# Later reads of the experts' names, a first matrix loaded in two halves, and more dummy products in a routed expert layer

## The chip, the core and the metric

The kernel runs on one core of one Trainium2 chip. Five engines work on their own instruction queues: PE (TensorE, matrix products), DVE (VectorE), ACT (ScalarE), POOL (GpSimd) and SP (SyncE, which here only starts transfers and reads registers). An instruction waits at the head of its queue until the semaphores it names are reached, and everything behind it on that engine waits with it. The metric is device microseconds for one execution of the whole program; lower is better.

## What is computed

Three stages follow each other: a linear attention, a dense mixture of four experts, and a routed mixture of eight experts. The change touches the third stage. Cut to what matters:

```python
def _moe2_ref(x, w_gate, w1, w2):            # x: 3072 x 384, 8 experts, 384 -> 1024 -> 384
    cap = N // E                             # 384 rows for each expert
    order = np.argsort(-(x @ w_gate).flatten())
    for idx in order:                        # greedy: best (row, expert) pair first
        tok, e = (int(idx) // E, int(idx) % E)
        if assigned[tok] >= 0 or counts[e] >= cap:
            continue
        assigned[tok] = e; counts[e] += 1
    for e in range(E):
        mask = assigned == e
        h = np.maximum(x[mask] @ w1[e], 0.0)
        out[mask] = h @ w2[e]
```

## The kernel before, in words

The dense stage ends at about 973 us of the span. Its 24 result tiles of 128 rows (`acc`) are written to a scratch tensor `x2d` in HBM by `finish` (L1221, on SP). The routed stage then works in eight **jobs**, one for each expert, in the order in which the experts fill up. A job gathers its 384 rows from `x2d` (three indirect gathers on POOL, L1515), turns them into `xT` with three groups of three PE transpositions (L1529; a copy on ACT, L1531, and a difference on DVE, L1532), then runs **up** (72 matmuls, lines 1133 to 1137, f from 0 to 7 with nine matmuls each) and **down** (72 matmuls, lines 1154 to 1158: three row blocks, in each f from 0 to 7 with three matmuls). Results leave by three scatters on POOL (L1647).

Each expert's two matrices come as 8 loads of 384 KB each: `w<-v1s` for up and `w<-v2s` for down, number f for step f. All of them stand at L1487 and are started by SP. Up's tiles have 9 buffers, down's have 8, so a load of the next expert's first matrix waits until the step of the running up that used its buffer is over.

Which expert comes next is found by the **routing**: rounds of counting products on PE (12 matmuls at L471), thresholds on DVE, and single small products (L502, lines 490 to 493, 567, 568, 598, 605). These are strewn among the matmuls of the jobs. A round first gives the expert's number (`worth`, tile `ev`), and some microseconds later the list of its rows (`index`, tile `idx`, L612). `name_job` (L1479) is called when `ev` has been written into the program: SP reads the number into a register (`value_load`, L1480, a TENSOR_LOAD) because the address of the expert's matrices depends on it. SP stands still there until DVE has really computed `ev`.

The order is fixed when the program is written. A planner keeps modelled clocks (`clk` for PE, `ready`, `act`, `dve`) and, after each matmul, decides by `tick1` and `tick2` whether a routing step, a load (`prepare(q, "loads")`) or a transposition (`prepare(q, "rows")`) is due. `load2(f)` of the running job is written at the start of its up's step f. A load of the next job's first matrix is written once `free(f)` holds: `ups`, the number of finished up steps of the running job, has reached `min(8, f + 4)`.

For the first job, POOL's gathers wait for all writes of `x2d`. All eight `w<-v1s` loads are written ahead of the last two of these writes, and the first `w<-v2s` load waits for the third gather. Until its rows arrive, PE is given **dummy products** (`keep_warm`, L1574, on the constant tile `tri`), as many as fit into the modelled time; the transpositions of the three row tiles are due at 5.5, 6.5 and 7.5 us after the modelled start of the gathers.

Of the kernel before, what the change touches and what calls it, by code (L numbers as in the profile page):

```python
# [814 lines left out]
def main(ctx, tc, A, out, C, stepwise):  # L815
# [659 lines left out]
    job, known = [], []  # L1475
    clk, ready, act, dve = [0.0], [0.0, 0.0], [0.0], [0.0]
    at_job = {"j": -1, "ups": 8}

    def name_job(ev):  # L1479
        e = nc.sync.value_load(ev[0:1, 0:1], min_val=0, max_val=E2 - 1)  # L1480
        jb = {"e": e, "n": len(known), "split": 0}
        known.append(jb)

        def load(which, f):
            src = C["v%ds" % which]
            w = slot(which, f)
            d = nc.sync.dma_start(flat(w), src[bass.ds(e, 1), :, 768 * f:768 * f + 768].rearrange("o p n -> p (o n)"))  # L1487
            if jb["n"] == 0 and which == 2 and f == 0:

                tc.add_manual_dep(d.ins, jb["got"].ins.name,  # L1490
                                  mybir.DependencyInfo(mybir.DependencyClass.Sync, mybir.DependencyReason.DATA),
                                  reason="rows first")

        def load1(f):
            load(1, f)
            jb["split"] = f + 1

        jb["load2"] = lambda f: load(2, f)
        before = jb["n"] - 1
        free = lambda f: at_job["j"] > before or (at_job["j"] == before and at_job["ups"] >= min(8, f + 4))  # L1500
        jb["loads"] = [(lambda f=f: load1(f), lambda f=f: free(f), lambda: 0.0) for f in range(8)]

    def start_job(idx):
        jb = known[len(job)]
        jb["idx"] = idx
        job.append(jb)
        if len(job) == E2:
            nc.vector.tensor_copy(C["again"], route.bad[0:1])
        xg = []

        def fetch():
            jb["t"] = clk[0]
            for i in range(3):
                t = wk.tile([128, D], F32, name="acc", bufs=8)
                jb["got"] = nc.gpsimd.indirect_dma_start(  # L1515
                    out=t, out_offset=None, in_=x2d, in_offset=bass.IndirectOffsetOnAxis(ap=idx[:, i:i + 1], axis=0))
                xg.append(t)
        if rows_there:
            fetch()
        else:  # L1520
            jb["fetch"] = fetch

        def tr(i):
            if i == 0:
                jb["xT"] = wk.tile([128, 2, 3, 768], F32R, name="xT", bufs=2)
            xT = jb["xT"]
            p = psum.tile([128, 3, 128], F32, name="at", bufs=4)
            for d in range(3):
                nc.tensor.transpose(p[:, d, :], xg[i][:, 128 * d:128 * d + 128], ident)  # L1529
            cs = slice(128 * i, 128 * i + 128)  # L1530
            nc.scalar.activation(xT[:, 0, :, cs], p, AF.Copy)  # L1531
            nc.vector.tensor_sub(xT[:, 1, :, cs], p, xT[:, 0, :, cs].bitcast(F32))  # L1532
            clk[0] += 0.43
            act[0] = max(act[0], clk[0] + 0.12) + 0.37
            dve[0] = max(dve[0], act[0] + 0.05) + 0.5

        if jb["n"]:
            jb["rows"] = [(lambda: [tr(i) for i in range(3)], lambda: len(xg) == 3, lambda: jb["t"] + 8.5)]
        else:
            jb["rows"] = [(lambda i=i: tr(i), lambda: len(xg) == 3, lambda i=i: jb["t"] + 5.5 + i) for i in range(3)]  # L1540

    def pop_route(q=None):
        if q is None:
# [45 lines left out]

    def tick2(j):  # L1590
        tick1(j)
        for q in known[j:j + 2]:
            prepare(q, "loads")
        for q in job[j:j + 2]:
# [30 lines left out]
    for j in range(E2):  # L1625
        while len(job) <= j:
            pop_route()
        jb = job[j]
# [79 lines left out]
```

## Time and profile before

| what | us |
|---|---|
| median of 3 runs | 1257.57 (1252.29 to 1263.45) |
| the profiled execution, its own time | 1255.2 |
| its span, in which all rows below lie | 1253.1 |
| end of the dense stage's last matmul | 973 |
| jobs 0 to 7, first to last matmul | 985.9 to 1238.7 |

Times in rows are microseconds from the span's start. In a row of the timeline, the number in brackets is how long the engine sat idle just ahead of that instruction, and what ended the wait. Matmuls of 384 columns are listed with about 0.33 us each, but they are pipelined and follow each other at about 0.17 us.

### The profile page before, as it was taken

Reading aid. Unit: us, or ns where it says so; the run is one execution under the profiler, and the core shown is the slowest. Engines: PE = TensorE matmul, PEld = TensorE weight load, DVE = VectorE, ACT = ScalarE, POOL = GpSimd, SP = SyncE. Lnnn points to the kernel's source line nnn. Section 1 sums busy time; section 2 is a strip of 40 time slices with the busy share of each in tenths; the row PEclk is TensorE's granted clock in tenths of the full one; section 3 lists DMA queues with packets and bytes.
Section 4 is the critical chain, followed back from the end, with each engine's and each line's share of the span. In section 5 each row is a group of like instructions: output and inputs, shape, how many; then the busy total and the mean of one; then the engine's idle time right before and its main releaser. Section 6 shows DMA issues by size and latency. Waiting matters only on the chain.

```text
span 1253.1 us, 21217 instructions
## 1 busy us (share of the span) xinstructions
PE 1218.4 (97%) x7961; PEld 1176.3 (94%) x7961; DVE 626.9 (50%) x1667; ACT 286.9 (23%) x608; POOL 413.0 (33%) x413
## 2 busy tenths in 40 slices
PE   8999999999999999999999999999999899989995
PEld 8899999999999999999999999999998778988995
DVE  7643333366333335853333377388756566653320
ACT  1322222212222222322222222222120111212221
POOL 5555454502444443244444423122100112312210
PEclk8999999999999999999999999999999899999998
DMA  6676555335777776578777645889522467647770
GB/s 248 214 274 218 189 190 189 140 120 164 244 265 248 267 246 219 173 251 276 240 276 238 230 148 194 284 272 305 175 86 86 152 245 259 215 161 254 281 284 25
DMA packets 95930, 267.65 MB, mean 214 GB/s; under 512 B 11328, under 2 KB 15552, under 8 KB 95680
## 3 DMA queue, kind: packets, MB, share of 16 engines
q1 hardware_dynamic: 92736, 256.67, 59.4%
q0 software_dynamic: 3072, 9.44, 2.2%
q8 instruction: 67, 1.10, 0.4%
q14 instruction: 55, 0.45, 0.1%
HBM read 181.13 MB, written 84.93 MB: 212 GB/s over the span
## 4 chain that ended last, share of the span: by engine, by line
PE 86%; issue 5%; DMA 3%; DVE 2%; POOL 2%; SPq 1%; ACT 0%; POOLq 0%; DVEq 0%
PE mm L1133 13%; PE mm L1154 12%; PE mm L1135 12%; PE mm L1158 12%; PE mm L1156 12%; PE mm L1137 12%; PE at L995 3%; PE at L963 2%; DMA w<-v2s 2%; PE at L991 2%; PE at L1012 1%; PE at L471 1%; PE at L1028 1%; POOL out_dram L1647 1%; SPq L1487 1%
## 5 line engine op out<-in xcount | busy, mean ns | idle before, releaser
L1154 PE MATMUL mm<-w,h 128*128 128x384 f32 x939 | 322.1, 343 | 9.4 <-DMA w<-v2s 8.3
L1133 PE MATMUL mm<-xT,w 128*128 128x384 f32 x960 | 328.8, 342 | 1.3 <-ACT xT L1531 1.3
L1135 PE MATMUL mm<-xT,w 128*128 128x384 f32 x960 | 323.5, 337 | 0.0
L1137 PE MATMUL mm<-xT,w 128*128 128x384 f32 x960 | 322.8, 336 | 0.0
L1158 PE MATMUL mm<-w,h 128*128 128x384 f32 x939 | 316.2, 337 | 0.0
L1156 PE MATMUL mm<-w,h 128*128 128x384 f32 x939 | 315.7, 336 | 0.0
L1141 ACT ACTIVATE h<-mm 128x384 fp32r<-128x384 f32 x313 | 153.9, 492 | 532.9 <-PE mm L1137 472.0
L1142 DVE SCALAR_TENSOR_TENSOR h<-mm,h 128x384 fp32r<-128x384 f32 x313 | 173.3, 555 | 200.3 <-ACT h L1141 199.4
L1073 POOL TENSOR_TENSOR ws<-raw,ws 128x384 fp32r<-128x384 f32 x128 | 135.4, 1063 | 345.3 <-ACT ws L1072 334.7
L1154 PEld LDWEIGHTS mm<-w,h 128*128 128x128 f32 x939 | 176.9, 188 | 12.3 <-issue 11.4
L1133 PEld LDWEIGHTS mm<-xT,w 128*128 128x128 f32 x960 | 181.1, 189 | 5.6 <-ACT xT L1531 2.0
L1135 PEld LDWEIGHTS mm<-xT,w 128*128 128x128 f32 x960 | 181.0, 189 | 0.7 <-DVE xT L1532 0.3
L1137 PEld LDWEIGHTS mm<-xT,w 128*128 128x128 f32 x960 | 180.9, 188 | 0.2
L1156 PEld LDWEIGHTS mm<-w,h 128*128 128x128 f32 x939 | 176.9, 188 | 0.2
L1158 PEld LDWEIGHTS mm<-w,h 128*128 128x128 f32 x939 | 176.7, 188 | 0.4
L1170 DVE SCALAR_TENSOR_TENSOR scr<-acc,wg 128x384 f32<-128x384 f32 x192 | 118.7, 655 | 0.1
L1418 DVE SCALAR_TENSOR_TENSOR acc<-mm,dp,acc 128x384 f32<-128x384 f32 x72 | 44.4, 616 | 107.2 <-PE mm L1158 107.1
L1073 POOL TENSOR_TENSOR w<-raw,w 128x384 fp32r<-128x384 f32 x60 | 61.2, 1039 | 96.4 <-ACT w L1072 96.4
L1072 ACT ACTIVATE ws<-raw 128x384 fp32r<-128x384 f32 x128 | 65.1, 520 | 97.5 <-DMA v2s<-ws 52.5
L1647 POOL DMA_INDIRECT out_dram<-acc,idx x24 | 24.4, 1017 | 153.7 <-ACT acc L1645 141.0
L1515 POOL DMA_INDIRECT acc<-x2d,idx x24 | 24.6, 1024 | 143.5 <-DVE Q L513 86.0
L995 PE MATMUL at<-rkv,am 128*128 128x48 f32 x352 | 50.7, 272 | 0.2 <-DVE am L974 0.2
(250 smaller groups left out, 1034.4 us busy)
## 6 DMA issues: line engine op xcount, KB each, us to landing
w<-w1s SPq DMA_DIRECT2D x72, 384.0 KB, 4.5
w<-w2s SPq DMA_DIRECT2D x72, 384.0 KB, 6.7
raw<-in_v_dram SPq DMA_DIRECT2D x64, 384.0 KB, 4.5
v1s<-ws SPq DMA_DIRECT2D x64, 384.0 KB, 3.1
v2s<-ws SPq DMA_DIRECT2D x64, 384.0 KB, 3.2
w<-v1s SPq DMA_DIRECT2D x64, 384.0 KB, 6.3
w<-v2s SPq DMA_DIRECT2D x64, 384.0 KB, 5.6
rkv<-in_rkv_dram SPq DMA_DIRECT2D x22, 640.0 KB, 6.5
```

The source lines that it names most:

```text
L995: nc.tensor.matmul(y[:, 48 * h:48 * h + 48], st[ck][:, s, p, :], v[:, 48 * h:48 * h + 48], start=not c, stop=bool(s) or not c)
L1072: nc.scalar.activation(w[:, 0], r, AF.Copy)
L1073: engine.tensor_tensor(w[:, 1], r, w[:, 0].bitcast(F32), op=OP.subtract)
L1133: nc.tensor.matmul(p, w[:, 0, ks], xh, start=(k == 0), stop=False)
L1135: nc.tensor.matmul(p, w[:, 0, ks], xl, start=False, stop=False)
L1137: nc.tensor.matmul(p, w[:, 1, ks], xh, start=False, stop=(k == 2))
L1141: nc.scalar.activation(h[:, 0], p, AF.Relu)
L1142: nc.vector.scalar_tensor_tensor(h[:, 1], p, 0.0, h[:, 0].bitcast(F32), op0=OP.max, op1=OP.subtract)
L1154: nc.tensor.matmul(p, h[:, 0, ts], w[:, 0], start=(f == 0), stop=False)
L1156: nc.tensor.matmul(p, h[:, 0, ts], w[:, 1], start=False, stop=False)
L1158: nc.tensor.matmul(p, h[:, 1, ts], w[:, 0], start=False, stop=(f == FB - 1))
L1170: nc.vector.scalar_tensor_tensor(scr[e % 2], x, 1.0, wg[:, e], op0=OP.mult, op1=OP.mult, accum_out=to[:, e:e + 1])
```

## The change

It has three parts. First, `name_job` no longer reads the number at once: it puts `ev` on a list with a due time, which is the modelled PE clock plus 2.5 us (for the first expert plus 0), and `take_names`, called after each matmul group, writes the read once the clock is there, or when a job must start. Second, the first job's `w<-v1s` loads 4 to 7 are written only after the gathers exist, and the wait for the third gather moves from the first `w<-v2s` load to `w<-v1s` load 4. Also, `free` wants `min(8, f + 6)` finished up steps instead of `min(8, f + 4)`. Third, the first job's transpositions are due at 7.6, 8.85 and 10.1 us instead of 5.5, 6.5 and 7.5, so that more dummy products stand ahead of them.

```diff
+    names = []
+
     def name_job(ev):
+        names.append((ev, clk[0] + (2.5 if known or names else 0.0)))
+        take_names()
+
+    def take_names(n=0):
+        while names and (clk[0] >= names[0][1] or len(known) < n):
+            take_name(names.pop(0)[0])
+
+    def take_name(ev):
         e = nc.sync.value_load(ev[0:1, 0:1], min_val=0, max_val=E2 - 1)
...
-            if jb["n"] == 0 and which == 2 and f == 0:
+            if jb["n"] == 0 and (which, f) == (1, 4):
                 tc.add_manual_dep(d.ins, jb["got"].ins.name,
...
-        free = lambda f: at_job["j"] > before or (at_job["j"] == before and at_job["ups"] >= min(8, f + 4))
-        jb["loads"] = [(lambda f=f: load1(f), lambda f=f: free(f), lambda: 0.0) for f in range(8)]
+        free = lambda f: at_job["j"] > before or (at_job["j"] == before and at_job["ups"] >= min(8, f + 6))
+        jb["loads"] = [(lambda f=f: load1(f), lambda f=f: free(f) and (f < 4 or "got" in jb or jb["n"]), lambda: 0.0)
+                       for f in range(8)]
 
     def start_job(idx):
+        take_names(len(job) + 1)
         jb = known[len(job)]
...
-            jb["rows"] = [(lambda i=i: tr(i), lambda: len(xg) == 3, lambda i=i: jb["t"] + 5.5 + i) for i in range(3)]
+            jb["rows"] = [(lambda i=i: tr(i), lambda: len(xg) == 3, lambda i=i: jb["t"] + 7.6 + 1.25 * i) for i in range(3)]
...
     def tick2(j):
         tick1(j)
+        take_names()
         for q in known[j:j + 2]:
```

What this does to the instruction order is shown at three places. The first is SP's queue where the first job's loads meet the last two writes of `x2d`. Before, the eighth load of the first matrix stands ahead of the two writes; behind them come loads of the second matrix, the first of which waits for the third gather (DMASW2):

```order
L1487 DMA w_9505<-v1s 128x768 [waits DMAHW1_49,PE_49]
L1221 DMA x2d<-acc 128x384 [waits DMAHW2_49,DVE_49]
L1221 DMA x2d<-acc 128x384 [waits DMAHW3_49,DVE_49]
L1487 ISA
L1487 DMA w_9762<-v2s 128x768 [waits DMAHW4_49,DMASW2_49,PE_49]
```

In the changed kernel the two writes stand behind the fourth load of the first matrix, and the fifth one waits for the third gather:

```order
L1498 DMA w_9478<-v1s 128x768 [waits DMAHW5_49,PE_49]
L1221 DMA x2d<-acc 128x384 [waits DMAHW6_49,DVE_49]
L1221 DMA x2d<-acc 128x384 [waits DMAHW7_49,DVE_49]
L1498 ISA
L1498 DMA w_9600<-v1s 128x768 [waits DMAHW0_49,DMASW2_49,PE_49]
```

So four loads of 384 KB each have moved from ahead of the last writes to behind the gathers, and the second matrix's loads stand behind these four.

The second place is SP's queue in job 3, around the read of the sixth expert's number. Before, loads 5 to 7 of job 3's second matrix stand behind the read (the last `v2s` row ahead of it is load 4, the one behind it is load 5):

```order
L1487 DMA w_11401<-v1s 128x768
L1487 ISA
L1487 DMA w_11403<-v2s 128x768
L1480 TENSOR_LOAD ev
L1480 ISA x2
L1487 ISA
L1487 DMA w_11461<-v1s 128x768
L1487 ISA
L1487 DMA w_11463<-v2s 128x768
```

In the changed kernel six `v2s` loads, 0 to 5, stand ahead of the read, and only loads 6 and 7 behind it, each with one load of the next expert's first matrix in front:

```order
L1498 DMA w_11494<-v2s 128x768
L1491 TENSOR_LOAD ev
L1491 ISA x2
L1498 ISA
L1498 DMA w_11518<-v1s 128x768
L1498 ISA
L1498 DMA w_11520<-v2s 128x768
L1498 ISA
L1498 DMA w_11557<-v1s 128x768
L1498 ISA
L1498 DMA w_11559<-v2s 128x768
```

The read has moved down past one load of the second matrix, one load of the next expert's first matrix has moved behind it, and load 7 is now the fourth load behind the read instead of the sixth.

The third place is PE's queue where the first job's first row tile (`acc`) is turned. Before, one dummy product stands between the third count and the transposition:

```order
L471 LDWEIGHTS ch
L471 MATMUL at<-oh,ch 40x62
L1574 LDWEIGHTS tri
L1574 MATMUL mm<-tri 128x128
L1529 MATMUL at<-ident,acc 128x128 [waits DMASW0_49]
```

In the changed kernel 24 dummy products and the small product L502 stand there, and the next count follows the first transposition, where before it stood inside the first up:

```order
L1587 LDWEIGHTS tri
L1587 MATMUL mm<-tri 128x128
L1542 MATMUL at<-ident,acc 128x128 [waits DMASW0_49,PE_49]
L1542 MATMUL at<-ident,acc 128x128 x2
L471 LDWEIGHTS ch
L471 MATMUL at<-oh,ch 40x64 [waits DVE_49]
```

Up to the first matmul of job 0 there are now 37 dummy products after the third count instead of 12, and one whole count and one set of lines 490 to 493 have moved from job 0's up to the wait for the rows. In jobs 0 to 3 the later routing steps stand earlier too: L567, just ahead of which DVE makes the number of the next expert, stands in job 0 after matmul 35 of up instead of 52, and in job 3 after matmul 56 instead of 65. From job 4 on the steps stand where they stood, to within a few matmuls. In job 0 the loads 4 to 7 of the second matrix stand behind the read, where before 5 to 7 did; in job 4 loads 6 and 7 stand behind both reads, where before 3 to 7 did, and load 7 is the fourth load behind them instead of the ninth.

## Rows read from the trace of the kernel before

**Rows 1.** The page's busy times by engine, whole span.
```profile
PE 1218.4 (97%) x7961; PEld 1176.3 (94%) x7961; DVE 626.9 (50%) x1667; ACT 286.9 (23%) x608; POOL 413.0 (33%) x413
```
**Rows 2.** PE's waits, 940 to 1253: total us, times, longest us.
```profile
PE mm L1154 <- DMA w<-v2s: 8.3, 6, 2.1
PE at L1529 <- DMA acc<-x2d,idx: 3.2, 1, 3.2
```
**Rows 3.** Stretches of 2 us: length, busy us (count) by engine, clock, DMA share, GB/s.
```profile
980.00:982.00 2.00, 0.09 (x1) 0.09 (x2) 0.00 (x0) 0.00 (x0) 1.70 (x2) 1.00 0.53 131
990.00:992.00 2.00, 2.00 (x11) 1.54 (x9) 0.57 (x2) 0.49 (x1) 0.00 (x0) 0.50 0.69 269
```
**Rows 4.** The chain that ended last, in order of time: start us, us, what.
```profile
973.33 0.62 DVE acc L1418
...
978.51 3.36 DMA acc<-x2d,idx
...
985.90 0.69 PE mm L1133
...
992.89 0.19 PE mm L1133
```
**Rows 5.** Timeline of SP, 960 to 990: start us, us of the group, transfer.
```profile
963.89 4.93 SPq L1487 DMA_DIRECT2D w<-v1s  x8
968.93 5.37 SPq L1221 DMA_DIRECT2D x2d<-acc  x2
984.39 2.70 SPq L1487 DMA_DIRECT2D w<-v2s  x5
```
**Rows 6.** Transfers issued in 957 to 963: count, KB each, us to landing.
```profile
x2d<-acc SPq DMA_DIRECT2D x1, 192.0 KB, 1.9
```
**Rows 7.** Timelines of DVE and POOL, 1015 to 1017: a later list and its gather.
```profile
1015.73 0.17 DVE L612 TENSOR_SCALAR idx<-xs 128x3 int32<-128x3 f32 x1
...
1016.17 0.98 POOL L1515 DMA_INDIRECT acc<-x2d,idx  x1 [2.55 <-DVE xl L504]
```
**Rows 8.** Timeline of PE, 965 to 1025: a group of dummy products, the third count.
```profile
973.57 1.46 PE L1574 MATMUL mm<-tri 128*128 128x128 bf16 x23
...
978.00 0.51 PE L471 MATMUL at<-oh,ch 128*40 128x62 bf16 x12 [0.28 <-DVE oh L448]
```
**Rows 9.** SP's own waits, 940 to 1253: total us, times, longest us.
```profile
SPq L1480 <- DVE bd L546: 75.9, 6, 18.0
```
**Rows 10.** Timeline of SP in job 3, around the read of a number.
```profile
1090.34 0.33 SPq L1487 DMA_DIRECT2D w<-v2s  x1
1105.04 0.34 SPq L1487 DMA_DIRECT2D w<-v1s  x1
```
**Rows 11.** The chain that ended last, 1000 to 1160: loads, issue and landing.
```profile
1107.81 7.95 DMA w<-v2s
...
1143.33 7.96 DMA w<-v2s
```
**Rows 12.** Timeline of PE in job 3: up's first, down's first, two waits, and later.
```profile
1092.26 0.35 PE L1133 MATMUL mm<-xT,w 128*128 128x384 f32 x1
...
1107.86 0.33 PE L1154 MATMUL mm<-w,h 128*128 128x384 f32 x1
...
1113.92 0.41 PE L1154 MATMUL mm<-w,h 128*128 128x384 f32 x1 [2.12 <-DMA w<-v2s]
...
1115.89 0.66 PE L1154 MATMUL mm<-w,h 128*128 128x384 f32 x1 [1.20 <-DMA w<-v2s]
...
1119.23 0.33 PE L1154 MATMUL mm<-w,h 128*128 128x384 f32 x1
```
**Rows 13.** One stretch of 1 us behind these waits; columns as in rows 3.
```profile
1116.00:1117.00 1.00, 1.00 (x4) 1.00 (x5) 0.00 (x0) 0.00 (x0) 0.00 (x0) 0.50 1.00 396
```
**Rows 14.** Timeline of PE: first matmul of job 7's up and of its down.
```profile
1213.89 0.33 PE L1133 MATMUL mm<-xT,w 128*128 128x384 f32 x1
...
1226.37 0.33 PE L1154 MATMUL mm<-w,h 128*128 128x384 f32 x1
```

## The prediction

> **What bounds the kernel now.** I read the page's busy times first: PE is busy for 1218.4 us, 97% of the span [rows 1], so only what makes PE wait or run slowly can matter. The change starts where the dense stage ends, at about 973 us, so I then read PE's own waits from there on. Two causes hold nearly all of them: 8.3 us in six waits of down's matmuls for loads of the second matrix, and 3.2 us for the first job's rows [rows 2]. Next come stretches with their granted clock: while PE waits for the first rows it is busy 0.09 of 2 us, and ten microseconds later its clock is 0.50, the 1.2 GHz level [rows 3]. The chain that ended last tells when the rows come [rows 4], and the timeline of SP why loads are late: SP stands still 75.9 us, six times, at the read of an expert's number [rows 9]. The rest of the eight jobs is matmuls that follow each other at 0.173 us (12.48 us for 72, [rows 14]) and the routing's own work; both stay.
>
> **Part 1: the first job's rows.** The last result tile is ready at 973.95 (973.33 plus 0.62) and its write to the scratch tensor goes out at once; the gathers can start only when it has landed. The first starts at 978.51, 4.6 us later [rows 4]. The write's cover is plain: all eight loads of the first matrix were issued from 963.89 to 968.82, just ahead of it [rows 5]. A write of the same size with nothing else under way landed after 1.9 us [rows 6]. Where a gather waits for its list alone, it starts 0.27 us after it (1015.90 to 1016.17, [rows 7]). With four loads instead of eight ahead, the earliest gather is 973.95 + 1.9 + 0.27 = 976.1, a gain of 2.4 us; the least is nothing, if POOL and not the write sets the start. I take 1.8, nearer to the write's row, since POOL has several semaphores to look at and not one.
>
> PE's order allows it. The third count ends at 978.51; behind it the changed queue holds 37 dummy products of 0.063 (1.46 us for 23, [rows 8]), 2.3 us, another count, 0.5, and two groups of transpositions and seven small products, about 1: the third tile's turn comes at 982.4. Its transpositions, ACT's copy and the start of up take about 1.2, so up can begin at 983.6 at the earliest, 2.3 sooner than the 985.90 of rows 4. With the rows 1.8 sooner and the transpositions at full clock I take 2.1 us, between 0 and 2.3.
>
> **Part 2: the dummy products.** Before, PE idles for 3.2 us until the rows land at 981.87 (978.51 plus 3.36). The 23 dummy products added ahead of the first transposition fill 1.5 of it, and 1.8 us go with the earlier rows; the count and the small products that moved here fill what is left between the tiles. What the lost clock costs: from 985.90 to 992.89 stand 15 matmuls of up and the count that now moves [rows 4], 6.99 us; 15 matmuls at 0.173 take 2.60. Of the 4.4 us between, 0.4 stays, since up's second matmul still waits for DVE's difference of the last tile. So 4.0 us, between 0 and 4.4. The products themselves cost nothing, since PE would wait there; if the rows come later, still more of them are hidden.
>
> The Trainium skill (TensorE: Matmul & The Clock Gate, Part 1) says that the engine is throttled by default, that only activity releases it, and that the moment of the change differs from run to run. The trace agrees with the first half, by the 0.50 of rows 3; no run here shows the second yet, and it is a rival below.
>
> **Part 3: the reads of the names.** In job 3 SP issues load 4 of the second matrix at 1090.34 and then stands at the read; the next load goes out at 1105.04 [rows 10]. Loads 5 to 7 follow as the second, fourth and sixth of ten in a row. Load 7 goes out at 1107.81 and lands 7.95 later [rows 11]; down, which began at 1107.86, waits 2.12 for load 6 and 1.20 for load 7 [rows 12]. Job 4's load 7 takes 7.96 [rows 11], and job 0 has the like. A matmul is listed with 0.33 and paced at 0.173, so each gap is 0.16 longer than the wait that the row shows: 8.3 + 6 x 0.16 = 9.3 us. Behind job 3's gaps the clock falls to 0.50 [rows 13]: nine matmuls from 1115.89 to 1119.23 [rows 12] take 3.3 us instead of 1.6, 1.7 more.
>
> After the change, loads 0 to 5 of job 3 stand ahead of the read. The number itself comes nine matmuls sooner, 1.6 us, so the first load behind the read goes out 11.2 us after up's start instead of 12.8 (1105.04 less 1092.26). Load 7 is the fourth of the burst; the fourth of the old one, load 6, was there at 1113.9, 8.9 us after it began. So load 7 lands 20.1 us after up's start. Down begins at 15.6 (1107.86 less 1092.26) and wants load 7 after 21 matmuls and a count, 3.6 + 0.5, at 19.7. That leaves a wait of 0.4, or 2.0 if the number comes no sooner. In job 4 load 7 becomes the fourth behind the reads instead of the ninth. In job 0 it is the sixth, but the number comes 17 matmuls sooner: read at about 6.2 us of up, load 7 there 10.7 later, at 16.9, and wanted at 12.5 + 3.6 or later. I leave 0.5 us for all three jobs, between 0 and 4. The gain is 8.8 us (5.3 to 9.3), and 1.7 for the clock (0 to 1.7).
>
> The Trainium skill (DMA: Bandwidth & Descriptors, Queues, rings and completion order) says that one queue's descriptors are consumed in ring order. By that alone a load would not be held up by those behind it, and nothing would be left of the waits: 0.5 us more gain. The row is against it: the sixth of ten landed 10.7 us after the burst began (1115.76), the fourth after 8.9, so later loads take their share. I go by the row.
>
> What does the later read cost? Behind it now stand the loads of the next expert's first matrix, and they are held back two steps more. In job 3 ten loads leave within 5.5 us of the read, and if the last lands as far behind the sixth as twice the step from fourth to sixth, that is 14.4 us after 1105.04, at 1119.4. The next up cannot begin before 1120.3 (1107.86 plus 12.48), and it wants load 7 only 63 matmuls later, 10.9 us. So nothing; the cover is some 5 us for loads 2 to 4 and more for the others. The first job's loads 4 to 7 wait for the rows: SP issued its first load behind the third gather at 984.39 [rows 5], now at about 982.6. Load 4 is wanted after 36 matmuls and a count, at 983.8 + 6.7 = 990.5; 6 us to landing, more than a burst's second load needed in job 3, leave 1.9. The second matrix's loads behind them are wanted 12.5 us after up's start at the earliest. Also nothing.
>
> **The sum.** 2.1 + 4.0 + 8.8 + 1.7 = 16.6 us. Job 1's transpositions, which now have three matmuls behind them, may win half a microsecond; I set it against small new waits of PE on DVE. The profiled execution took 1255.2 us for a span of 1253.1; it becomes 1238.6. The median of the runs, 1257.57, is 2.4 above it, and from there the forecast is 1241.0. That is 1.3% faster; 1%, about 12.6 us, is what a measurement of this kernel can tell from no change.
>
> **The rivals.**
> - *The clock falls all the same, or the rows are no earlier.* For it: one gap of 3.2 us was enough, and the stretch stays a mix of short work and waits. Against it: at the end of that gap the clock still stood at 1.00 [rows 3], so shorter ones should be harmless. It loses the 4.0 and half of the 2.1: gain 11.5, 1246. A moment of change that differs from run to run, as the skill has it, would do this in some runs.
> - *The reads are not late enough.* The planner counts 0.161 us for a matmul where the trace has 0.173, and SP runs ahead of the place where its instructions are written: it waited up to 18.0 us at a read [rows 9], and 2.5 us more of modelled time moves one or two loads past it. If half of the 9.3 stays, and the slow clock, the gain is 16.6 - 4.2 - 1.7 = 10.7 us, 1247.
> - *Both*: gain 5.6 us, 1252.
> - *The first matrices come late.* If the next expert's loads, now behind load 7 and the read, miss its up, PE waits there in up to six jobs, at 5 us each and 1.7 for the clock: 40 us, less the 16.6, or 1281. It decides once a read comes over 5 us later against its job than now. Nothing points there; the routing moves forward.
>
> **How the numbers follow.** Forecast 0.60, which with the bounds of its terms and the spread of the runs reaches from 1236 to 1247; clock or rows 0.15; reads 0.13; both 0.07; late first matrices 0.05. The range 1234 to 1253 leaves out the last case and some edges, under 2 in 10. Faster by over 1% (below 1245): 0.56 of the forecast's case and a third of the next two, 0.10, make 0.66. Slower by over 1% is 0.04, within 1% the other 0.30.
>
> **What would show it.** Right: the first gather starts between 976 and 977.5, the stretches from 978 to 994 all stand at clock 1.00, job 0's first matmul is at about 983.8, and PE's waits for second-matrix loads are under 1.5 us in total. SP's time at the reads may stay large, for the reads only move to where less stands behind them. Wrong in part 1: a gather still near 978.5. Wrong in part 3: down's steps 6 and 7 waiting again in jobs 0, 3 and 4. The forecast as a whole fails if up's first matmuls (L1133) wait for first-matrix loads.

## The result and the profile after

The changed kernel takes 1241.38 us (median of 4 runs, 1240.10 to 1241.85), the kernel before 1257.63 beside it. The ratio is 0.9868 with a 95% interval from 0.9824 to 0.9913, so it is 1.3% faster, and 1241.0 was forecast. The profiled execution went from 1255.2 to 1240.1 us and its span from 1253.1 to 1238.1.

The page's busy times for the changed kernel, beside [rows 1]:

```profile
PE 1213.8 (98%) x7986; PEld 1174.4 (95%) x7986; DVE 629.5 (51%) x1667; ACT 287.2 (23%) x608; POOL 412.0 (33%) x413
```

PE has 25 instructions more and is busy 4.6 us less: the dummy products are added, and after the first 50 us (below) no matmul runs at the slow clock any more. PE's waits from 940 us on (total us, times, longest us), the first three of the list, beside [rows 2]:

```profile
PE at L1542 <- DMA acc<-x2d,idx: 2.4, 3, 1.5
PE mm L1133 <- ACT xT L1544: 0.6, 1, 0.6
PE at L502 <- DVE xT L1545: 0.4, 1, 0.4
```

The 8.3 us of waits for second-matrix loads are gone altogether. What is left for rows looks like the old 3.2 us and is not: one wait of three is for the rows of job 0, the longest, 1.49 us, for the rows of job 5, which are turned during up of job 4 (below). The two stretches that answer to [rows 3] (length, busy by engine, clock, DMA share, GB/s):

```profile
980.00:982.00 2.00, 1.63 (x28) 1.29 (x25) 1.69 (x4) 0.49 (x1) 0.57 (x1) 1.00 0.63 180
990.00:992.00 2.00, 2.00 (x23) 1.61 (x22) 1.50 (x10) 0.11 (x2) 0.00 (x0) 1.00 0.98 366
```

PE is busy for 1.63 of the 2 us that it idled through before, and the clock ten microseconds later is 1.00 (2.4 GHz) instead of 0.50 (1.2 GHz). The chain that ended last around the first gathers (start us, us, what), beside [rows 4]:

```profile
973.50 0.62 DVE acc L1418
...
976.71 0.18 DVE xl L504
976.91 1.16 POOL acc L1528
...
978.37 3.50 DMA acc<-x2d,idx
982.00 0.52 PE at L1542 x3
```

The first gather starts at 976.91, 3.41 us behind the start of the last result tile's step instead of 5.18. The chain puts this start down to a step of DVE that ends at 976.89, 0.02 us ahead (`xl`, a threshold of the next search). That is a coincidence. The list that the gather needs was there almost 7 us earlier, by DVE's timeline:

```profile
969.95 0.17 DVE L612 TENSOR_SCALAR idx<-xs 128x3 int32<-128x3 f32 x1
```

And in the kernel before, the same step of DVE stands at almost the same time, while the gather began 1.8 us after its end, at 978.51:

```profile
976.54 0.17 DVE L504 TENSOR_REDUCE xl<-at 128x1 f32<-128x8 f32 x1 [0.27 <-PE at L502]
```

What the gather follows is the landing of the last write of `x2d`. Eight of the fourteen traces in the table below tell when it lands; here are the changed kernel and the one with the dummies alone (count, KB, us from issue to landing):

```profile
x2d<-acc SPq DMA_DIRECT2D x1, 192.0 KB, 1.9
```

```profile
x2d<-acc SPq DMA_DIRECT2D x1, 192.0 KB, 3.6
```

In the four of these eight that have the split (changed, changed again, split alone, split and dummies) the write lands 2.5 us behind the start of the tile's step and the gather starts at 3.4. In the four without it (reads, holding back, dummies, more dummies, each alone) the write lands 4.0 to 4.3 us behind it and the gather starts at 5.1 to 5.4. The gather stands 0.9 us behind the landing with the split and 1.1 us without, so the write sets its start in both. SP's timeline at the same place, beside [rows 5]:

```profile
964.07 2.14 SPq L1498 DMA_DIRECT2D w<-v1s  x4
967.90 6.58 SPq L1221 DMA_DIRECT2D x2d<-acc  x2
982.79 2.48 SPq L1498 DMA_DIRECT2D w<-v1s  x4
```

Four loads stand ahead of the write, four behind the gathers. SP's reads, beside [rows 9], and its queue in job 3, beside [rows 10]:

```profile
SPq L1491 <- DVE bd L546: 56.8, 6, 14.5
```

```profile
1079.65 4.88 SPq L1498 DMA_DIRECT2D w<-v2s  x6
...
1097.23 0.33 SPq L1498 DMA_DIRECT2D w<-v2s  x1
...
1098.35 0.33 SPq L1498 DMA_DIRECT2D w<-v2s  x1
...
1112.52 14.57 SPq L1498 DMA_DIRECT2D w<-v2s  x6
```

Six loads of the second matrix go out ahead of the read instead of five, and load 7 leaves 13.3 us after up began (at 1085.02) instead of 15.6. PE's timeline in the same job and the next, beside [rows 12], and the transfers issued from 1112 to 1122 (count, KB each, median us to landing):

```profile
1100.58 0.33 PE L1154 MATMUL mm<-w,h 128*128 128x384 f32 x1
...
1115.97 0.34 PE L1133 MATMUL mm<-xT,w 128*128 128x384 f32 x1
...
1120.17 0.82 PE L1542 MATMUL at<-ident,acc 128*128 128x128 f32 x6
1122.47 0.52 PE L1542 MATMUL at<-ident,acc 128*128 128x128 f32 x3 [1.49 <-DMA acc<-x2d,idx]
```

```profile
w<-v2s SPq DMA_DIRECT2D x5, 384.0 KB, 6.2
acc<-x2d,idx POOLq DMA_INDIRECT x3, 7.2
```

Down of job 3 runs through without a wait, 15.39 us instead of 20.59. But behind it stands a wait that was not there before: the rows of job 5 land late. Their gathers are issued from 1112.11 to 1115.11, and from 1112.52 to 1115.18 SP issues five second-matrix loads of job 4. The one of the three gathers whose landing the trace tells takes 7.2 us (7.6 in the repeat), where in the kernel before the same job's took 4.2 and 4.9.

**Where the 15.1 us come from.** The kernel from the start of the last result tile's step (L1418, 973.33 before, 973.50 after) to the start of the last down matmul I call the stretch. It went from 265.34 to 251.12 us, 14.2 less. Behind it the span has 14.4 us before and 13.5 after, 1.0 less (in the changed kernel run again it is 14.3); the start is 0.17 later. Within the stretch, 1.9 come ahead of up's first matmul, 3.0 in up of job 0, and 9.3 from down of job 0 on. All experiments are compared by these parts, for a reason that the runs themselves gave: the work ahead of the stretch, which no edit is about, varies by more than most edits bring. Two executions show it, the first 50 us of the kernel with the dummies alone and of the changed kernel run again:

```profile
0.00:50.00 50.00, 44.45 (x385) 40.35 (x386) 38.67 (x80) 12.56 (x26) 34.76 (x39) 1.00 0.76 274
```

```profile
0.00:50.00 50.00, 46.19 (x335) 43.35 (x336) 32.36 (x69) 9.43 (x19) 25.29 (x32) 0.80 0.67 239
```

At clock 1.00 PE gets through 385 instructions, at 0.80 through 335, and the last result tile is there at 965.59 in the one and at 973.49 in the other. The ten timed runs of the first lie between 1239.5 and 1253.5 us. Each kernel has one trace, so the stretch is one measurement too: the changed kernel's two traces differ by 1.1 us in it.

### The profile page after: what moved, and what is told of

Same layout as the page of the kernel before. It is cut to its first block, busy times and chain, and to the rows that moved or that the text cites. A ratio compares the mean times of both kernels' runs of the same rounds, so it can differ in the third digit from the quotient of the medians.

```text
span 1238.1 us, 21280 instructions
## 1 busy us (share of the span) xinstructions
PE 1213.8 (98%) x7986; PEld 1174.4 (95%) x7986; DVE 629.5 (51%) x1667; ACT 287.2 (23%) x608; POOL 412.0 (33%) x413
## 4 chain that ended last, share of the span: by engine, by line
PE 89%; issue 4%; DMA 2%; DVE 2%; POOL 1%; ACT 0%; POOLq 0%; DVEq 0%; ACTq 0%
PE mm L1133 13%; PE mm L1154 13%; PE mm L1156 13%; PE mm L1158 13%; PE mm L1135 13%; PE mm L1137 12%; PE at L995 3%; PE at L963 2%; PE at L991 2%; DMA acc<-x2d,idx 1%; PE at L1012 1%; PE at L471 1%; PE at L1028 1%; POOL out_dram L1661 1%; PE at L968 1%
## 5 line engine op out<-in xcount | busy, mean ns | idle before, releaser
L1418 DVE SCALAR_TENSOR_TENSOR acc<-mm,dp,acc 128x384 f32<-128x384 f32 x72 | 44.4, 617 | 105.6 <-PE mm L1158 105.4
```

## The experiments

The table has for each kernel its median and ratio, and then from its trace: the time from the last result tile's step to up's first matmul, the length of up of job 0, the time from down of job 0 to the last matmul, their sum (the stretch), and PE's waits for second-matrix loads (total us, times). Each ratio is against runs of the kernel before beside it, whose medians lie between 1255.5 and 1259.9 us, so the medians of different rows are not to be set against each other to the microsecond.

| kernel | median us | ratio, 95% | to up | up of job 0 | rest | stretch | waits |
|---|---|---|---|---|---|---|---|
| before | 1257.6 | | 12.57 | 17.87 | 234.90 | 265.34 | 8.3, 6 |
| reads alone | 1245.91 | 0.9892 (0.9836 to 0.9949) | 12.54 | 16.92 | 226.83 | 256.29 | 0.8, 1 |
| holding back alone | 1246.97 | 0.9930 (0.9897 to 0.9964) | 12.61 | 17.80 | 229.09 | 259.50 | 3.2, 2 |
| split alone | 1257.45 | 0.9991 (0.9964 to 1.0018) | 11.34 | 16.53 | 233.57 | 261.44 | 7.1, 6 |
| dummies alone | 1247.96 | 0.9935 (0.9901 to 0.9968) | 13.72 | 16.08 | 228.43 | 258.23 | 3.5, 4 |
| more dummies alone | 1253.22 | 0.9971 (0.9954 to 0.9989) | 13.21 | 16.42 | 232.56 | 262.19 | 4.9, 3 |
| split and dummies | 1246.54 | 0.9925 (0.9900 to 0.9949) | 11.32 | 14.81 | 228.96 | 255.09 | 3.2, 4 |
| all but the reads | 1245.81 | 0.9897 (0.9877 to 0.9916) | 12.14 | 14.82 | 226.58 | 253.54 | 1.6, 2 |
| all but the dummies | 1248.16 | 0.9910 (0.9888 to 0.9932) | 11.18 | 17.78 | 227.77 | 256.73 | 0 |
| all but the split | 1245.95 | 0.9893 (0.9867 to 0.9919) | 13.36 | 14.81 | 227.68 | 255.85 | 0 |
| all but holding back | 1246.61 | 0.9902 (0.9874 to 0.9929) | 12.12 | 14.81 | 228.07 | 255.00 | 0 |
| changed | 1241.38 | 0.9868 (0.9824 to 0.9913) | 10.67 | 14.83 | 225.62 | 251.12 | 0 |
| changed, again | 1242.08 | 0.9883 (0.9862 to 0.9904) | 11.35 | 14.82 | 226.06 | 252.23 | 0 |
| changed, later rows | 1241.22 | 0.9872 (0.9850 to 0.9893) | 11.30 | 14.80 | 223.89 | 249.99 | 0 |

### Each part alone

The four parts of the change (its second part is two edits, the split of the first job's loads and the holding back) were put into the kernel before one at a time. The reads of the names alone:

```diff
...
+        names.append((ev, clk[0] + (2.5 if known or names else 0.0)))
+        take_names()
...
```

> Only the later reads of the names are taken over; loads, due times and the holding back of the next first matrix stay as before. Theory (the reads set the waits of down): PE's waits for second-matrix loads fall from 8.3 us to under 2, the slow clock in job 3 goes, the first gather stays near 978.5 and the clock still falls behind it; span some 9 to 11 us shorter than before. Rival (it is the holding back of the next expert's first matrix that clears the queue): the waits stay above 4 us and the span is less than 5 us shorter.

The holding back of the later first matrices alone:

```diff
-        free = lambda f: at_job["j"] > before or (at_job["j"] == before and at_job["ups"] >= min(8, f + 4))
+        free = lambda f: at_job["j"] > before or (at_job["j"] == before and at_job["ups"] >= min(8, f + 6))
```

> Only the limit of finished up steps for the next expert's first matrix goes from f + 4 to f + 6. Theory (the reads set the waits): waits for second-matrix loads stay between 3 and 7 us, since in job 3 loads 5 to 7 still stand behind the read; span 1 to 6 us shorter. Rival (the holding back alone does it): waits under 1.5 us and the span about 10 us shorter.

The split of the first expert's first matrix alone:

```diff
-            if jb["n"] == 0 and which == 2 and f == 0:
+            if jb["n"] == 0 and (which, f) == (1, 4):
...
-        jb["loads"] = [(lambda f=f: load1(f), lambda f=f: free(f), lambda: 0.0) for f in range(8)]
+        jb["loads"] = [(lambda f=f: load1(f), lambda f=f: free(f) and (f < 4 or "got" in jb or jb["n"]), lambda: 0.0)
+                       for f in range(8)]
```

> Only four of the first matrix's eight loads are held behind the rows. Theory (the write of the last result tile stood behind the loads): first gather at about 977 instead of 978.5, PE's wait for the first rows down from 3.2 to about 1.6 us, job 0's first matmul 1.5 to 1.7 us earlier, and the clock still falls behind the gap, so the span is about 2 us shorter. Rival (the earlier rows alone keep the clock, the dummy products are not needed): the clock stays at 1.00 up to 994 and the span is 5 to 6 us shorter.

The dummy products alone:

```diff
-            jb["rows"] = [(lambda i=i: tr(i), lambda: len(xg) == 3, lambda i=i: jb["t"] + 5.5 + i) for i in range(3)]
+            jb["rows"] = [(lambda i=i: tr(i), lambda: len(xg) == 3, lambda i=i: jb["t"] + 7.6 + 1.25 * i) for i in range(3)]
```

> Only the due times of the first job's transpositions are later, so that 37 dummy products instead of 12 stand behind the third count. Theory (dummy products keep the clock): first gather still near 978.5, a gap of under 2 us ahead of the rows, clock 1.00 up to 994, 4 to 5 us shorter at the start of job 0's down; waits for second-matrix loads remain in jobs 3 and 4. Rival (the earlier rows keep the clock): the clock falls as before and the span is less than 2 us shorter.

The stretch gets shorter by 9.05, 5.84, 3.90 and 7.11 us, together 25.9, where the whole change brings 14.2. So the parts draw on the same loss. Where they overlap is in the column of waits: of the 8.3 us, the reads alone leave 0.8, the holding back alone 3.2, and the dummies alone, which have nothing to do with any load, leave 3.5. For the first two the first theories hold in the waits; the reads alone brought 9.05 us in the stretch but 7.7 in the span, where 9 to 11 were expected. The reads' own waits on SP and PE's waits for the second matrix, with the reads alone:

```profile
SPq L1491 <- DVE bd L546: 47.9, 6, 11.8
```

```profile
PE mm L1154 <- DMA w<-v2s: 0.8, 1, 0.8
```

The split alone shortens the way to up by 1.2 us, as the theory of the write wants. But its clock falls all the same, at a wait of 1.3 us for the rows instead of 3.2:

```profile
984.00:986.00 2.00, 1.69 (x12) 1.22 (x10) 1.34 (x3) 0.76 (x2) 0.00 (x0) 0.50 0.31 41
```

The 3.9 us of its stretch hold some chance, too. In job 3 SP's loads of the second matrix stand at the same times after up's start as before, within 0.01 us, and still PE waits 0.41 us for load 6 where it waited 2.12:

```profile
1112.62 0.41 PE L1154 MATMUL mm<-w,h 128*128 128x384 f32 x1 [0.41 <-DMA w<-v2s]
```

So a single one of these waits can differ by 1.7 us without any edit to it. And the dummies alone do not hold the clock either. In that kernel the rows still come late, PE waits 2.0 us for them behind its last dummy product, and up begins at 979.31 (all there is 7.7 us earlier, by the start above). Both theories of this run missed: the clock falls, and yet the stretch is 7.1 us shorter:

```profile
980.00:982.00 2.00, 2.00 (x7) 2.00 (x8) 0.89 (x4) 0.00 (x0) 0.00 (x0) 0.50 0.90 278
```

### Each part left out

From the changed kernel one part at a time was undone. All but the reads, which go back to the place where the name is written:

```diff
...
-        names.append((ev, clk[0] + (2.5 if known or names else 0.0)))
-        take_names()
...
```

> The changed kernel with the reads of the names put back to where the numbers are written; everything else as changed. Measured from the last result tile's DVE step to the last matmul (265.3 us before, 251.1 changed). Theory (reads, holding back and an earlier routing all clear the same waits of down, so they overlap): waits for second-matrix loads come back only in part, 1 to 4 us, stretch 252.5 to 256. Rival (the reads alone do it, and the other parts only seemed to in single runs): waits above 6 us, stretch above 258.

All but the dummy products:

```diff
-            jb["rows"] = [(lambda i=i: tr(i), lambda: len(xg) == 3, lambda i=i: jb["t"] + 7.6 + 1.25 * i) for i in range(3)]
+            jb["rows"] = [(lambda i=i: tr(i), lambda: len(xg) == 3, lambda i=i: jb["t"] + 5.5 + i) for i in range(3)]
```

> The changed kernel with the first job's transpositions due at 5.5, 6.5 and 7.5 us again, so 12 dummy products behind the third count instead of 37. Theory (the clock needs both the earlier rows and the dummy products): the gather stays 3.4 us behind the last result tile's DVE step, the clock falls to 0.50 behind the gap, job 0's up takes 16 us or more instead of 14.8; stretch 254 to 256. Rival (with the earlier rows the clock holds): clock 1.00 throughout and stretch under 252.5.

All but the split:

```diff
-            if jb["n"] == 0 and (which, f) == (1, 4):
+            if jb["n"] == 0 and which == 2 and f == 0:
...
-        jb["loads"] = [(lambda f=f: load1(f), lambda f=f: free(f) and (f < 4 or "got" in jb or jb["n"]), lambda: 0.0)
-                       for f in range(8)]
+        jb["loads"] = [(lambda f=f: load1(f), lambda f=f: free(f), lambda: 0.0) for f in range(8)]
```

> The changed kernel with all eight loads of the first matrix ahead of the last writes of the scratch tensor again. Theory (the write stands behind the loads): the gather starts 5.1 to 5.3 us behind the last result tile's DVE step instead of 3.4, PE has a gap of about 2 us in spite of 37 dummy products, the clock falls to 0.50 and job 0's first matmul comes about 3 us later; stretch 254.5 to 257. Rival (the dummy products alone keep the clock): clock 1.00 throughout, stretch about 253.

All but the holding back:

```diff
-        free = lambda f: at_job["j"] > before or (at_job["j"] == before and at_job["ups"] >= min(8, f + 6))
+        free = lambda f: at_job["j"] > before or (at_job["j"] == before and at_job["ups"] >= min(8, f + 4))
```

> The changed kernel with the next expert's first matrix held back to f + 4 finished up steps again instead of f + 6. Theory (the waits are cleared by the reads and the earlier routing already): waits for second-matrix loads under 1.5 us, stretch 250.5 to 253. Rival (the holding back is needed): waits above 3 us, stretch above 254.

The stretch is longer than the changed kernel's by 2.4, 5.6, 4.7 and 3.9 us, and by 1.1 less each against its repeat. The part that was to carry more than half of the gain, the reads, is the one that is missed least: with the other three in place the waits for the second matrix come to 1.6 us. What is missed most is the dummies, and there 3.0 of the 5.6 us are the clock: up of job 0 takes 17.78 us, as long as before, and the stretch is 0.7 us above the first theory's range. Without the split the gather starts 4.7 us behind the tile (5.1 to 5.3 were expected), and otherwise the first theory holds. Without the holding back the waits stay at 0, as the first theory has it, but the stretch missed it by 2 us: the rows of jobs 3 and 5 wait 3.1 us where the changed kernel's wait 2.2, and the rest was not followed.

Part of the 2.4 and of the 3.9 is a loss of 1.5 us at the start (0.8 against the repeat) that no theory had. PE's timeline without the reads:

```profile
981.88 0.17 PE L502 MATMUL at<-W,dg 8*128 8x8 bf16 x1 [0.95 <-issue]
...
984.45 0.51 PE L471 MATMUL at<-oh,ch 128*40 128x64 bf16 x12 [1.05 <-DVE oh L448]
```

PE stands for 0.95 us at a small product behind a count, and nothing in the profile ends that wait ("issue"); the next count then waits for DVE, and the way to up is 12.14 us. The kernel without the holding back has the same two waits, 0.94 and 1.05, and 12.12; the changed kernel has neither in either of its traces. Why stays open.

### Split and dummies together, and more dummies

Neither the split nor the dummies alone kept the clock, and without either it fell. So the next kernel has these two and nothing else:

```diff
...
+            if jb["n"] == 0 and (which, f) == (1, 4):
...
+            jb["rows"] = [(lambda i=i: tr(i), lambda: len(xg) == 3, lambda i=i: jb["t"] + 7.6 + 1.25 * i) for i in range(3)]
```

> The kernel before with half of the first matrix behind the rows and with the longer row of dummies; names are read and loads are held back as before. Theory that these two together are the whole gain at the start: first gather 3.4 us and up's first matmul 10.7 to 12.1 us behind the result tile, clock 1.00 from 974 to 994, and of the down matmuls' waits for second-matrix loads 3.5 us stay, as with the dummies alone; the stretch is 255 to 256 (265.3 before, 251.1 with everything). Rival, that the reads and the holding back count at the start too: the clock falls and the stretch is 258 or more.

The first theory holds. The way to up and up itself take 26.13 us, the changed kernel run again 26.17: the gain at the start is these two alone. The clock and the waits:

```profile
984.00:986.00 2.00, 1.27 (x7) 0.78 (x6) 1.89 (x7) 0.49 (x1) 0.00 (x0) 1.00 0.90 242
```

```profile
PE mm L1154 <- DMA w<-v2s: 3.2, 4, 1.2
PE at L1530 <- DMA acc<-x2d,idx: 1.8, 3, 0.9
```

From down of job 0 on, this kernel has won 5.9 of the 9.3 us as well, with the reads where they were; the reads and the holding back add the last 2.9 to 3.3. The rival cause, that the dummies themselves hold the clock, was tried with so many of them that they go on until the late rows of the unchanged gathers:

```diff
-            jb["rows"] = [(lambda i=i: tr(i), lambda: len(xg) == 3, lambda i=i: jb["t"] + 5.5 + i) for i in range(3)]
+            jb["rows"] = [(lambda i=i: tr(i), lambda: len(xg) == 3, lambda i=i: jb["t"] + 9.4 + 1.25 * i) for i in range(3)]
```

> The kernel before with the first job's rows due at 9.4, 10.65 and 11.9 instead of 5.5, 6.5 and 7.5, so that dummy products go on until the rows of the unchanged gathers land; nothing else. Dummies up to 7.6, 8.85 and 10.1 alone left a gap of 1.95 us and the clock fell. Theory that the gap alone makes the clock fall: the gap is under 1 us, the clock stays at 1.00 from 974 to 994, up of job 0 is 3 to 4 us shorter than with the shorter row of dummies, and the stretch is 254 to 255 (258.2 with the shorter row). Rival, that the dummies themselves do not hold the clock: it falls to 0.50 again with hardly a gap, and the stretch is 258 to 259. Third: the dummies run past the rows, up begins up to 1.5 us later than 12.6 behind the result tile, and takes back that much.

This missed its aim: they did not reach, since the first two tiles' turns come later too and the second tile's still finds no rows. PE's waits and the clock behind them:

```profile
PE mm L1154 <- DMA w<-v2s: 4.9, 3, 2.3
PE at L1529 <- DMA acc<-x2d,idx: 2.4, 2, 1.3
```

```profile
990.00:992.00 2.00, 2.00 (x9) 2.00 (x8) 0.59 (x2) 0.06 (x1) 0.00 (x0) 0.56 0.00 0
```

A wait of 1.3 us is left and the clock falls, as with the split alone. So whether dummies that fill the whole gap would hold it without earlier rows was not shown. The stretch is 4 us longer than with the shorter row of dummies, and the difference lies in the rest (232.56 against 228.43). The waits for the second matrix are 1.4 us of it; the other 2.7 were not followed further.

### Again, and with later rows

> The changed kernel once more, to see what of it repeats. Stretch means: from the start of the last result tile's step on DVE (L1418) to the start of the last down matmul (L1158). If the stretch is settled by the program, it is 251.1 us again within 0.5, up's first matmul stands 10.7 us behind the result tile, the clock is 1.00 from 974 to 994, no down matmul waits for a second-matrix load and the rows of job 4 wait 1.5 us again. If small shifts decide (rival), up's first matmul comes up to 1.5 us later, as in the runs without the reads and without the holding back (12.1), and the stretch is 252 to 253. The median should be 1241 by the first, up to 1244 by the second.

The clock, the missing waits and the rest repeat (226.06 against 225.62). The way to up does not: 11.35 instead of 10.67, because one gather lands 0.7 us later while everything ahead of it stands at the same time within 0.02 us. So the stretch, 252.2 us, is the rival's, and the waits and the clock are the first theory's. A difference of a microsecond in the stretch says nothing; the medians are 0.7 us apart.

The new waits for rows were tested by making the rows of jobs 1 to 7 due later (the 1.49 us that the expectation gives to job 4 are for job 5's rows, during job 4's up):

```diff
-            jb["rows"] = [(lambda: [tr(i) for i in range(3)], lambda: len(xg) == 3, lambda: jb["t"] + 8.5)]
+            jb["rows"] = [(lambda: [tr(i) for i in range(3)], lambda: len(xg) == 3, lambda: jb["t"] + 10.5)]
```

> The changed kernel with the rows of jobs 1 to 7 due 2 us later, 10.5 in place of 8.5 behind the start of their routing. The changed kernel's rows of jobs 3 and 4 wait 0.66 and 1.49 us for gathers that share the DMA engines with six loads. Theory: later rows find their gathers landed, nothing else is due meanwhile that needs them, and the stretch goes from 251.1 to about 249. Rival: what is queued behind the rows (the copies to xT, and the next up) then comes as much later, and the stretch stays at 251 or grows to 253 with a wait of up's first matmul for xT.

The waits are gone and the first theory's size is nearly right. PE's row waits, and the transpositions of job 5's rows, nine in one piece:

```profile
PE at L1542 <- DMA acc<-x2d,idx: 0.8, 1, 0.8
```

```profile
1125.72 1.14 PE L1542 MATMUL at<-ident,acc 128*128 128x128 f32 x9
```

The only wait left is job 0's. From down of job 0 on it takes 223.89 us, 1.7 and 2.2 less than the changed kernel's two traces. The median, 1241.22 against 1242.08, can't tell the two apart: the intervals of the ratios overlap, and in the profiled execution the last result tile came 3.5 us later than in the other. It is no slower, and not shown to be faster.

## Why the prediction was right, and where it was not

The median is right to 0.4 us, and the terms come out at 1.9 us for 2.1, 3.0 for 4.0, and 9.3 for the 8.8 and 1.7 together. That the sum agrees so well is partly luck: the stretch brought 14.2 us of the 16.6 (13.1 in the repeat), and beside the repeat the medians of before and changed are 13.4 us apart and not 16.2. One sentence of part 2 failed, and part 3 gave the reads too much.

**Part 1, the rows: right.** 2.1 us were forecast; it is 1.9, and 1.2 in the repeat. The gather moved by 1.8, as taken, and the write was indeed covered by loads: without the split the gather starts 4.7 to 5.4 us behind the tile in every kernel, with it 3.4. The write now lands 1.9 us after its issue, as in [rows 6]. What was too small is the 0.27 us that the gather was given behind it: it takes 0.9, so the gather starts 3.4 us behind the start of the tile's step, where the prediction's earliest (976.1) is 2.8. By taking 1.8 of its 2.4 the prediction left room for that; what fills the 0.9 us was not tested.

**Part 2, the clock: right in size, and right that both edits are needed.** From up's first to its sixteenth matmul it is 6.78 us before and 3.15 after (984.17 to 987.32), 3.6 saved of the 4.0 forecast. Another count of the routing moved into up further on and takes 0.6 back, so that up of job 0 is 3.0 shorter. The prediction fills the gap of 3.2 us from two sides, and each does about what it was to do: the split alone leaves a wait of 1.3 us, the dummies alone one of 2.0. The step that failed is the sentence that shorter gaps should be harmless, because the clock still stood at 1.00 at the end of the old one; by it either edit alone would have done. With the split alone, without the dummies and with more dummies PE waits 1.3 us for the first rows, and each time the clock falls behind it. It also falls in the other five kernels that wait longer there (1.9 to 3.2 us), and stays at 1.00 in the six whose waits ahead of the first up are 1.05 us or less each. Without the split it is back by the time up begins, so that up there takes 14.81 us all the same. The forecast came true because both edits together leave waits of 0.2 to 0.9 us for the rows, and neither does it alone. The length of a wait does not settle it everywhere: inside the jobs the clock stayed at 1.00 behind waits of 1.49 us (changed) and 1.61 (without the split), and in job 4 of the kernel before behind 1.71 and 1.02; yet in job 0 with the split alone it fell behind 1.21 and 1.19. The row of the 1.71 us and a stretch behind both waits:

```profile
1149.63 0.41 PE L1154 MATMUL mm<-w,h 128*128 128x384 f32 x1 [1.71 <-DMA w<-v2s]
```

```profile
1152.00:1154.00 2.00, 2.00 (x14) 2.00 (x13) 0.00 (x0) 0.49 (x1) 0.95 (x1) 1.00 1.02 388
```

The Trainium skill (TensorE: Matmul & The Clock Gate, Part 1) has the moment at which activity releases the throttle differ from run to run. No run here was made to test that; what differs here is the moment of the fall. With the reads alone the clock fell within the wait, with the holding back alone, at a wait of the same 3.0 us, only behind it:

```profile
980.00:982.00 2.00, 0.36 (x8) 0.17 (x4) 0.41 (x4) 0.00 (x0) 1.56 (x2) 0.96 0.02 6
```

```profile
980.00:982.00 2.00, 0.00 (x0) 0.00 (x0) 0.22 (x3) 0.00 (x0) 1.70 (x2) 1.00 0.26 46
```

**Part 3, the reads: the waits went, but not by the reads alone.** 8.8 us of waits and 1.7 of slow clock were forecast, 10.5; from down of job 0 on it is 9.3 (8.8 in the repeat). All six waits went, worth 9.3 with their pace, and job 3's down has no slow matmuls. The prediction put this down to the later reads, with an earlier number as a help in jobs 0 and 3. With split and dummies alone, the reads where they were, 5.1 of the 8.3 us were gone already. The earlier number is the reason in job 0: there the dummies moved a count and the small products behind it ahead of the first up, and the step of DVE that releases SP's read (L546) starts 5.84 us after up's start (990.68 less 984.84) instead of 12.74 (998.64 less 985.90). The two rows, before and with split and dummies:

```profile
998.64 0.15 DVE L546 TENSOR_TENSOR bd<-x 128x1 f32<-128x1 f32 x1
```

```profile
990.68 0.15 DVE L546 TENSOR_TENSOR bd<-x 128x1 f32<-128x1 f32 x1
```

Job 0's two waits, 2.3 us in the kernel before, are gone with that:

```profile
1008.78 0.41 PE L1154 MATMUL mm<-w,h 128*128 128x384 f32 x1 [1.06 <-DMA w<-v2s]
...
1010.75 0.41 PE L1154 MATMUL mm<-w,h 128*128 128x384 f32 x1 [1.21 <-DMA w<-v2s]
```

In job 3 the same step starts 12.07 us after up's start before (1104.33 less 1092.26), 10.97 in the changed kernel (1095.99 less 1085.02) and 10.96 with split and dummies (1097.22 less 1086.26): 1.1 us sooner, where 1.6 were reckoned. There 3.3 us of waits became 0.6, and how much of that the number did is not shown, since the split alone, with the number no sooner, got 1.7 of it by loads that happened to land sooner. The residue of 0.5 did not come. Load 7's own landing is not told; the loads just ahead of it and behind it in the burst landed 5.8 and 8.0 us after the burst's start, where the prediction took 8.9 from the fourth load of the old one, also of ten loads. So that row was no constant. The measured zero is what the rule on ring order, which the prediction weighs, would have given, but it comes as well from a burst that lands sooner, so it does not decide on the rule.

**What was missing: the next wait.** The prediction looked for what the later first matrices would do, and found rightly that they cost nothing: no up waits for them in any of these traces. It did not ask what the earlier second matrices and the earlier routing would collide with. It is the gathers: the rows of jobs 3 and 5 wait 0.66 and 1.49 us, about 2.5 with their pace, and up of job 4, in which the second of these waits stands, takes 17.33 us instead of 14.76 (0.8 of it a group of 24 small products that moved in from down). With the later rows these waits are gone and 1.7 to 2.2 us are won, so that is what they cost; that the loads beside the gathers made them late is argued from their times and was not tested by itself. In the stretch 14.2 us came where 16.6 were forecast, and these waits are about what lacks. The median hides it: 1.0 came back behind the last matmul, where nothing was forecast and where the repeat shows almost none of it, and the medians are 16.2 apart where the profiled executions are 15.1, since that of before was 2.4 under its median and that of after 1.3.

## What to carry to other kernels

When several edits aim at the same waits, a sum of their gains is not to be had: put each alone and leave each out, and look at what the waits come to. A load that is late behind a read is helped by whatever makes the number earlier, be it work that has nothing to do with loads. Look also at a stretch that an edit leaves alone: what differs there between two traces is the size of chance. And where a burst of loads is moved forward, ask which small transfer on another queue was using that hole.

## What the runs showed of the hardware

- A wait of PE of 1.3 us for the first rows, in work that is a mix of short products, was followed by a clock of 0.50 for 3 to 10 us (three kernels); waits of 0.95 and 1.05 us there, 2.6 us apart, were not (two kernels). Inside the jobs, where most of the work is matmuls of 384 columns, waits of 1.49 us, of 1.61 and of 1.71 and 1.02 were not either, while 2.12 and 1.20 (job 3 of the kernel before) and 1.21 and 1.19 (job 0 with the split alone) were.
- The clock of the first 50 us stands between 0.73 and 1.00 in these executions; with 1.00 the last result tile was there 8 to 11 us earlier than with 0.73 to 0.83.
- The first job's first gather took 3.2 to 3.4 us to land with no load beside it; a later job's gather beside five loads of 384 KB took 7.2 us, and 7.6 in the repeat.
- The first gather started 0.9 us behind the landing of the write that it waits for in four traces and 1.1 us in four others, while that write took from 1.8 to 3.6 us to land.
- A wait of 0.95 us ahead of one product, which nothing in the profile ends, came in two kernels at the same place and in the others not.
